# Attention and expert kernel: a prologue for one head and one batch, and the banks of the transposed groups from the scores' ring

## The chip, the cores and the metric

The kernel runs on one core of a Trainium2 chip. The metric is the device time of one execution in microseconds. Before the change the median of three runs is 740.85 us (740.27 to 741.19).

## The reference

Three stages, one behind the other, all in fp32:

```python
q_pool = q.reshape(B, H, S // 2, 2, D).mean(axis=3)          # B 2, H 8, S 1152, D 64
scores = softmax(1/sqrt(D) * q_pool @ k.transpose(0, 1, 3, 2))
x = (scores @ v) -> rows (b, s), columns (h, d)              # 1152 x 512
out = experts(x): top 2 of 8 by noisy logits, relu(x @ w1[e]) @ w2[e]
h = out @ w_in; result = (h * cos(h)) @ w_out                # 512 x 2048, 2048 x 512
```

The change touches the attention stage alone, and of it the preparation of q and k.

## The kernel before

TensorE multiplies in a fast form of fp32 that keeps fewer bits, so each operand is split into a high part (written in that form) and a low part (the rest), and a product is made of two or three matmuls.

**Row tiles.** Attention goes over 72 row tiles `n` (`tiles`, line 281): 4 pairs of heads `hp`, 2 heads `hl` in a pair, 9 tiles `t` of 128 pooled query rows. The 1152 rows of a head are batch 0 (tiles 0 to 3 and half of tile 4) and batch 1 (the other half of tile 4, tiles 5 to 8). A tile has 1152 keys, in three score banks of 384 columns. In iteration `n` of the main loop (line 880) TensorE makes the scores of tile `n + 1` (`s_bank`: two matmuls a bank, high q and low q; three or four for the tile across both batches), VectorE their negative maxima (`s_max`), ScalarE their exponentials (`s_exp`, which also sums them: an instruction of its own then reads the accumulator). For tile `n` TensorE transposes the exponentials (`t_pe`, three groups), ScalarE and VectorE split two of them (`t_hi`, `t_lo`), ScalarE and GpSimd the third (`t_pool`). The products with v wait in a list (`avq`) from which each iteration takes 9, or 6 where `t` is 2 to 4 (`NPOP`); a product is 256 or 320 columns wide.

The order on an engine is the order in which the code issues. ScalarE's order in an iteration is `t_hi` 0 and 1 of tile `n`, exponentials 0 and 1 of tile `n + 1`, `t_pool`'s copy, exponential 2, and then copies of whatever group stands at the end of the iteration. TensorE's is score banks 0 and 1, `t_pe` 0, score bank 2, `t_pe` 1, products, `t_pe` 2, products, the group at the end.

**Banks.** PSUM's eight banks are three rings: `s` of four (scores), `pt` of three (`tbank`, line 122: transposes), `pa` of one (products). A ring hands its banks out in turn, and a new user waits for the last reader of the bank's former user.

**The plan.** Head pairs are prepared while the pair before is worked on. `plan` (line 728) puts each step at an iteration: loads, `pool_q` (adds neighbouring rows of q, GpSimd), `q_group` and `k_group` (three transposes into one bank and a copy by ScalarE; issued at the end of an iteration), `q_split` and `k_split` (GpSimd), then `q_asm`, `l_asm`, `q_bd`, `k_asm` (transfers from SBUF to SBUF, all in SyncE's queue, that bring the parts to the partitions where the score matmuls want them). `kb` and `qd` are the block rows for the low part of the tile across both batches. At the end of some iterations stands instead a row group (`x_group`): the finished columns of the output are transposed, scaled and stored.

**The prologue** (lines 770 to 862) loads q and k of heads 0 and 1 in both batches: q of batch 0 for head 0 and head 1, k of batch 0 in six pieces, k of batch 1 in two, q of batch 1 in two. Ten matmuls (`warm`) run while the loads are under way. For batch 0 VectorE adds q, TensorE transposes q and k of both heads together (`q_front`, `k_direct`), ScalarE writes the high parts and VectorE the low parts, and three more copies bring head 0's q to the other 64 partitions. Then come the scores of tile 0, key groups of batch 1, the exponentials of tile 0, the scores of tile 1 and the rest of q for batch 1, with copies on VectorE and ScalarE in iterations 1 and 2, and 17 transfers.

Of the kernel before, what the change touches and what calls it, by code (L numbers as in the profile page):

```python
# [22 lines left out]
def attn_moe_cos_kernel(ctx, tc, q, k, v, w_gate, w_noise, noise, w1, w2, w_in, w_out, out):  # L23
# [174 lines left out]
    def k_tiles(hp, b):
        kk = [qk.tile([128, S], F32R, name="kt", bufs=5) for _ in range(2)]
        KT[hp, 0, b], KT[hp, 1, b] = kk  # L200
        return kk

    def load_qb(hl, b):
        if b == 0:
            QN[0, hl] = prep.tile([128, 18, 64], F32, name="qn", bufs=2)
        nc.sync.dma_start(QN[0, hl][b * 64:(b + 1) * 64], q[b, hl].rearrange("(p r) d -> p r d", r=18))

    def pool_qb(hl, b, eng):
        rs = slice(b * 64, b * 64 + 64)
        t = QN[0, hl][rs].rearrange("p (s r) d -> p s r d", r=2)  # L210
        eng.tensor_tensor(QP[0][rs, :, hl, :], t[:, :, 0, :], t[:, :, 1, :], op=OP.add)
# [3 lines left out]
    def q_front(j, b):  # L215
        QB[j] = p = tbank()
        rs = slice(b * 64, b * 64 + 64)
        for i in range(3):
            nc.tensor.transpose(p[:, i * 64:(i + 1) * 64], QP[0][rs, 3 * j + i].rearrange("p h d -> p (h d)"), ident[rs, rs])

    def q_part(t, b, j):
        return t[:, b * QB1:b * QB1 + SQ].rearrange("p (s c) -> p s c", c=9)[:, :, 3 * j:3 * j + 3]

    def q_hi(b, j, o):
        nc.scalar.activation(q_part(o, b, j), QB[j][:, 0:192].rearrange("p (i s) -> p s i", i=3), AF.Copy, scale=1.0 / 16.0)
# [502 lines left out]
    def plan():  # L728
# [5 lines left out]
        for hp in range(HP):  # L734
            n0 = 18 * hp
            for hl in range(2):
                for b in range(B):
                    s = n0 + 9 * hl + 5 * b
                    at(s - 7, load_v, hp, hl, b)
                    at(s - 3, split_v, hp, hl, b)  # L740
            if hp:
# [29 lines left out]
    pres = ExitStack()  # L771
    pro = pres.enter_context(tc.tile_pool(name="pro", bufs=1, side="right", reuse_waits="tile"))
    load_qb(0, 0)
    load_qb(1, 0)
    load_k(0, 0)
    load_k(0, 1, pro)
    load_qb(0, 1)
    load_qb(1, 1)
    warm(tbank, WQ)
    QP[0] = prep.tile([128, 9, 2, 64], F32, name="qp", bufs=1)  # L780
    QH = QS[0] = prep.tile([128, 1216], F32R, name="sh", bufs=2)
    QL[0] = prep.tile([128, 1216], F32R, name="ql", bufs=1)
    t = t0 = Q2[0, 0] = qk.tile([128, 1216], F32R, name="q2", bufs=3)
    L0 = QL2[0, 0] = qk.tile([128, 1216], F32R, name="l2", bufs=2)
    for i in range(3):
        z = slice(512 * i, min(512 * i + 512, 1216))
        nc.gpsimd.tensor_scalar(L0[64:128, z], ZERO[64:128, 0:z.stop - z.start], 1.0, 0.0, op0=OP.mult, op1=OP.add)
    for hl in range(2):
        pool_qb(hl, 0, nc.vector)
    for j in range(3):  # L790
        q_front(j, 0)
    kk = k_tiles(0, 0)
    kbank = [lambda: ps.tile([128, 512], F32, name="s", bufs=4)] * 2 + [lambda: ps.tile([128, 512], F32, name="pa", bufs=1)]
    kg = [k_direct(0, 0, j, kk, kbank[j]) for j in range(3)]
    for g in kg:
        next(g)
    for j in range(3):
        q_hi(0, j, QH)
        q_lo(0, j)
    c = slice(0, SQ)  # L800
    nc.scalar.activation(t[64:128, c], QH[0:64, c], AF.Copy)
    nc.vector.tensor_scalar(t[0:64, c], QH[0:64, c], 1.0, 0.0, op0=OP.mult, op1=OP.add)
    nc.gpsimd.tensor_scalar(L0[0:64, c], QL[0].bitcast(F32)[0:64, c], 1.0, 0.0, op0=OP.mult, op1=OP.add)
    for g in kg:
        next(g)
    next(kg[0])
    s_mm(0)
    QR = pro.tile([128, 1216], F32, name="qr")
    z = slice(SQ, QB1)
    nc.gpsimd.memset(QR[:, z], 0.0)  # L810
    nc.gpsimd.tensor_scalar(QH[:, z], QR[:, z], 1.0, 0.0, op0=OP.mult, op1=OP.add)
    for hl in range(2):
        pool_qb(hl, 1, nc.gpsimd)
    QN.clear()
# [8 lines left out]
    for g in kg[1:]:
        next(g)
    KN.pop((0, 0))
    for j in range(3):
        k_group(0, 1, j)
# [10 lines left out]
    for j in range(3):
        q_hi(1, j, QR)
        q_hi(1, j, QH)  # L840
    k_split(0, 1)
    c = slice(SQ, 1216)
    nc.gpsimd.tensor_tensor(QL[0][:, c], QR[:, c], QH.bitcast(F32)[:, c], op=OP.subtract)
    lo0 = QL[0].bitcast(F32)
    ev.setdefault(1, []).insert(0, (lambda: nc.vector.tensor_scalar(
        t0[0:64, c], QH[0:64, c], 1.0, 0.0, op0=OP.mult, op1=OP.add), ()))
    ev.setdefault(2, []).insert(0, (lambda: nc.vector.tensor_scalar(
        L0[0:64, c], lo0[0:64, c], 1.0, 0.0, op0=OP.mult, op1=OP.add), ()))
    ev.setdefault(2, []).insert(0, (lambda: nc.scalar.activation(t0[64:128, c], QH[0:64, c], AF.Copy), ()))
    k_asm_a(0, 1)  # L850
    q_asm(0, 1, False)
    l_asm(0, 1)
    for n in sorted(e for e in ev if e < 0):
        for f, a in ev[n]:
            if f != load_v:
                f(*a)
    pres.close()
    kbp.append(qes.enter_context(tc.tile_pool(name="kbp", bufs=1, reuse_waits="tile")))
    k_stack(0)
    k_asm_b(0, 1)  # L860
    nc.sync.dma_start(KB[0, 1].bitcast(F32)[0:64], KT[0, 1, 0].bitcast(F32)[64:128])
    q_bd(0, 1)
# [17 lines left out]
    for n in range(NTOT - 1):  # L880
        hp, hl, t = tiles[n]
        for f, a in ev.get(n, []):
            if f not in (q_group, k_group):
# [58 lines left out]
        fl = [(f, a) for f, a in ev.get(n, []) if f in (q_group, k_group)]  # L942
# [770 lines left out]
```

## Time and profile before

| | before |
|---|---|
| median of 3 runs | 740.85 us (740.27 to 741.19) |
| profiled execution | 739.14 us, its span 737.6 us |
| TensorE (PE) busy | 722.5 us, 98% of the span |
| VectorE (DVE), ScalarE (ACT), GpSimd (POOL) busy | 562.3, 528.8, 301.9 us |
| granted TensorE clock, mean | 0.999 of full speed |

The profile is one execution on the chip; times are microseconds from the start of its span. The ends of matmuls are modelled, so the spacing of their starts tells more than their lengths. A row ahead of which an engine sat idle names in brackets for how long, and what released it. The attention stage lasts until about 275 us; the experts and the last two products follow.

### The profile page before, as it was taken

The numbers are of one execution on the slowest core, as the hardware profiler recorded it, in microseconds if no ns is written. First come the engines' busy times: TensorE is split into PE (matmuls) and PEld (weight loads), VectorE is DVE, ScalarE is ACT, GpSimd is POOL, SyncE is SP. The second block draws the span as 40 slices with busy tenths as digits, with TensorE's granted clock in tenths as the row PEclk, the third lists the DMA queues.
The fourth block names the chain that finished last, engine by engine and source line by source line (L and its number), as shares of the span: only waits on it lengthen the run. The fifth ranks groups of instructions, "written<-read, shape, count | busy, mean of one in ns | idle before, by whom it ended". The sixth has DMA issues, their size and how long they took to land.

```text
span 737.6 us, 13760 instructions
## 1 busy us (share of the span) xinstructions
PE 722.5 (98%) x4803; PEld 673.9 (91%) x4803; DVE 562.3 (76%) x1161; ACT 528.8 (72%) x1200; POOL 301.9 (41%) x329
## 2 busy tenths in 40 slices
PE   6999999999999999999999999999999999999997
PEld 4899999999999989999999999999889989888885
DVE  5888788888878988879889887776677776556562
ACT  5999799979988964458777676766588665555443
POOL 5988867877977973212022021103187110000000
PEclk9999999999999999999999999999999999999999
DMA  9957756695665511798999999968353210010001
GB/s 207 244 94 183 184 130 147 163 237 106 161 140 146 179 44 29 248 314 295 363 371 328 334 345 330 329 233 286 119 171 97 85 29 1 1 44 0 1 1 60
DMA packets 75329, 125.02 MB, mean 169 GB/s; under 512 B 11950, under 2 KB 42030, under 8 KB 75254
## 3 DMA queue, kind: packets, MB, share of 16 engines
q1 hardware_dynamic: 68678, 101.92, 47.3%
q0 software_dynamic: 5568, 19.14, 7.4%
q10 hardware_dynamic: 1008, 3.02, 1.6%
q8 instruction: 40, 0.66, 0.4%
q14 instruction: 35, 0.29, 0.1%
HBM read 82.15 MB, written 20.33 MB: 139 GB/s over the span
## 4 chain that ended last, share of the span: by engine, by line
PE 90%; DVE 4%; ACT 3%; DMA 1%; issue 0%; SPq 0%; ACTq 0%; DVEq 0%
PE h L1145 20%; PE acc L1145 16%; PE acc L1177 11%; PE s L310 10%; PE pa L386 9%; PE pt L348 9%; PE t L1145 7%; PE pt L694 2%; PE t L1137 1%; PE pt L984 1%; PE t L1194 1%; PE pt L180 1%; DMA raw<-in_moe_w_dram 1%; DVE nm L324 1%; DVE el L365 1%; DMA qn<-in_q_dram 1%
## 5 line engine op out<-in xcount | busy, mean ns | idle before, releaser
L324 DVE TENSOR_REDUCE nm<-s 128x1 f32<-128x384 f32 x216 | 112.1, 551 | 23.4 <-PE s L310 21.8
L333 ACT ACTIVATE p<-s,nm 128x384 f32<-128x384 f32 x216 | 125.1, 583 | 2.8 <-DVE nm L326 1.5
L1145 PE MATMUL h<-xe,u 128*128 128x320 f32 (+5 forms) x768 | 120.1, 306 | 0.0
L1145 PEld LDWEIGHTS h<-xe,u 128*128 128x128 f32 x768 | 109.6, 188 | 0.5
L642 DVE TENSOR_TENSOR u<-raw,u 128x1024 fp32r<-128x1024 f32 x66 | 80.9, 1227 | 34.4 <-ACT u L641 33.6
L348 PE MATMUL pt<-ident,p 128*128 128x128 f32 x645 | 105.0, 272 | 0.0
L310 PE MATMUL s<-kt,q 128*128 128x384 f32 x240 | 88.8, 386 | 3.7 <-DVE kt L195 2.1
L348 PEld LDWEIGHTS pt<-ident,p 128*128 128x128 f32 x645 | 81.7, 140 | 5.7
L386 PE MATMUL pa<-eh,v 128*128 128x320 f32 (+1 forms) x279 | 86.5, 324 | 0.0
L641 ACT ACTIVATE u<-raw 128x1024 fp32r<-128x1024 f32 x73 | 77.1, 1057 | 10.3 <-DMA raw<-in_moe_w_dram 5.8
L361 ACT ACTIVATE eh<-pt 128x384 fp32r<-128x384 f32 x144 | 68.9, 501 | 20.3 <-PE pt L348 19.0
L386 PE MATMUL pa<-el,v 128*128 128x320 f32 (+1 forms) x279 | 82.4, 309 | 0.0
L372 POOL TENSOR_TENSOR el<-rw,eh 128x384 fp32r<-128x384 f32 x71 | 71.9, 1012 | 5.9
L365 DVE TENSOR_TENSOR el<-pt,eh 128x384 fp32r<-128x384 f32 x144 | 72.9, 547 | 1.0 <-ACT eh L361 0.9
L1177 PE MATMUL acc<-hh,u 128*128 128x320 f32 (+5 forms) x448 | 71.8, 302 | 0.1
L1145 PE MATMUL acc<-u,gh 128*128 128x512 f32 x216 | 66.9, 391 | 0.0
L310 PE MATMUL s<-kt,l 128*128 128x384 f32 x198 | 66.3, 337 | 0.0
L1177 PEld LDWEIGHTS acc<-hh,u 128*128 128x128 f32 x448 | 64.7, 188 | 0.4 <-ACT hh L1156 0.4
L1232 POOL DMA_DIRECT2D w_d<-dw x16 | 9.0, 563 | 130.5 <-DVE dw L1231 130.5
L371 POOL TENSOR_SCALAR eh<-rw 128x384 fp32r<-128x384 f32 x71 | 36.8, 518 | 42.0 <-ACT rw L369 39.7
L386 PEld LDWEIGHTS pa<-el,v 128*128 128x128 f32 x279 | 52.9, 190 | 0.0
L386 PEld LDWEIGHTS pa<-eh,v 128*128 128x128 f32 x279 | 52.8, 189 | 0.0
(292 smaller groups left out, 1605.9 us busy)
## 6 DMA issues: line engine op xcount, KB each, us to landing
raw<-in_moe_w_dram SPq DMA_DIRECT2D x64, 512.0 KB
raw<-in_moe_w_in_dram SPq DMA_DIRECT2D x16, 512.0 KB
raw<-in_moe_w_out_dram SPq DMA_DIRECT2D x16, 512.0 KB
w_d<-dw POOLq DMA_DIRECT2D x16, 512.0 KB, 5.4
raw<-w_d SPq DMA_DIRECT2D x13, 512.0 KB
vn<-in_v_dram SPq DMA_DIRECT2D x16, 288.0 KB
q<-sh SPq DMA_DIRECT2D x14, 304.0 KB
l<-ql SPq DMA_DIRECT2D x14, 304.0 KB
```

What stands on the lines that cost most here:

```text
L310: nc.tensor.matmul(o, l, r, start=(m == 0), stop=(m == len(mm) - 1))
L324: nc.vector.tensor_reduce(NM[n][:, i:i + 1], SB[n][i][:, 0:384], axis=AX.X, op=OP.max, negate=True)
L333: nc.scalar.activation(P[n][i], SB[n][i][:, 0:384], AF.Exp, bias=NM[n][:, 3:4], accum_out=SUMS[:, t, 2 * hp + hl, i:i + 1])
L348: nc.tensor.transpose(p[:, c], P[n][j][:, c], ident)
L361: nc.scalar.activation(t_dst(n, j)[0], t_src(n, j), AF.Copy)
L365: nc.vector.tensor_tensor(el, t_src(n, j), ef, op=OP.subtract)
L372: nc.gpsimd.tensor_tensor(el, rw, ef, op=OP.subtract)
L386: nc.tensor.matmul(st["p"][:, 0:w], V2[hp, hl, b][:, VC[c] if hp + b else c, :], (EH, EL)[s][:, c, EB[g]:EB[g] + w], start=(c == 0 and s = ...
L641: nc.scalar.activation(b[:, 0], r, AF.Copy)
L642: st_w["lo"].tensor_tensor(b[:, 1], r, b.bitcast(F32)[:, 0], op=OP.subtract)
L1145: nc.tensor.matmul(o, l, r, start=first and i == 0, stop=last and i == len(seq) - 1)
L1177: nc.tensor.matmul(ACC[e, d][:, 0:CAPS[e]], w[:, i, 128 * d:128 * d + 128], r[:, 0:CAPS[e]], start=f == 0 and r is hh and i == 0, stop=f = ...
```

## The change

Part one: the prologue prepares head 0 alone, first its batch 0. The four loads are q of batch 0, k of batch 0, q of batch 1, k of batch 1 (each 288 KB). The added rows of q are written twice beside each other, so that one transposition fills all 128 partitions, and ScalarE and VectorE write high and low parts straight to their places (`pool_p`, `q_tr`, `q0_hi`, `q0_lo`). The keys of batch 0 are transposed 64 columns at a time into the lower partitions (`k0_tr`, `k0_part`). Behind the scores of tile 0 follow batch 1's q, and batch 1's keys (`k0b_copy`, `k0b_split`, four transfers). Head 1's q and k are loaded in the prologue, and prepared in iterations 1 to 9: `pool_h1` at 1, key groups at 1, 2 and 3, `k_split` at 4, q groups (`q1_group`) at 4, 5 and 6 with their low parts on VectorE one iteration later (`late`), eight transfers (`k1_asm`) at 6 and six (`k1_bd`) at 9. Some steps of pair 1 move with it: its first key load from 2 to 4, its second q group from 6 to 7, and the split of v for batch 1 from 2 to 5. The warming matmuls are 11, and use the matrix of ones for both operands.

Part two: key groups (`k_group`), q groups of pairs 2 and 3 and of head 1 of pair 0, and all row groups but the last two take their bank from the ring `s` of four instead of `pt`.

The core of the diff; definitions of helpers that only move data as told above are left out:

```diff
@@ q_group
-        p = tbank()
+        p = ps.tile([128, 512], F32, name="s", bufs=4) if hp > 1 else tbank()
@@ k_group
-            KS[hp, b] = prep.tile([128, 1216], F32, name="st", bufs=1)[:, 0:S]
-        p = tbank()
+            KS[hp, b] = prep.tile([128, 1216], F32, name="st", bufs=1)[:, 0:S] if hp else XS0
+        p = gbank()
...
+    def pool_p(hl, rs, cs, eng):
+        t = QN[0, hl][rs].rearrange("p (s r) d -> p s r d", r=2)
+        o = QP[0, hl][rs, cs]
+        eng.tensor_tensor(o[:, :, 0, :], t[:, cs, 0, :], t[:, cs, 1, :], op=OP.add)
+        if eng is nc.vector:
+            nc.scalar.activation(o[:, :, 1, :], o[:, :, 0, :], AF.Copy)
+        else:
+            eng.tensor_scalar(o[:, :, 1, :], o[:, :, 0, :], 1.0, 0.0, op0=OP.mult, op1=OP.add)
...
+    def gbank():
+        return ps.tile([128, 512], F32, name="s", bufs=4)
...
+    def q1_group(j):
+        cs = slice(3 * j, 3 * j + 3)
+        q_tr(1, slice(0, 128), cs, ("h", j))
+        src = QB["h", j][:, 0:384].rearrange("p (i b s) -> p b s i", i=3, b=2)
+        for b in range(2):
+            nc.scalar.activation(q0_out(Q2[0, 1], b, cs), src[:, b], AF.Copy, scale=1.0 / 16.0)
+        late.append(lambda: [nc.vector.scalar_tensor_tensor(...) for b in range(2)])
...
+    def k0b_copy():
+        KS[0, 0] = t = XF[:, 1280:1920]
+        nc.gpsimd.memset(t[HI, 512:640], 0.0)
+        pa, pb = tbank(), tbank()
+        k_tr(1, 0, pa)
+        nc.scalar.activation(t[:, 0:384], pa[:, 0:384], AF.Copy)
+        k_tr(1, 1, pb)
+        nc.scalar.activation(t[:, 384:512], pb[:, 0:128], AF.Copy)
+        nc.scalar.activation(t[LO, 512:640], pb[LO, 128:256], AF.Copy)
...
@@ x_group
-        p = tbank()
+        p = ps.tile([128, 512], F32, name="s", bufs=4) if (hp, g) < (HP - 1, 2) else tbank()
@@ plan
-                    at(s - 3, split_v, hp, hl, b)
+                    at(5 if s == 5 else s - 3, split_v, hp, hl, b)
-                at(m + 2, load_k, hp, 0)
+                at(m + (4 if hp == 1 else 2), load_k, hp, 0)
-                    at(m + (3 + 2 * d, 5 + d, 6 + d)[j], q_group, hp, j)
+                    at(m + (3 + 2 * d, 5 + 2 * d, 6 + d)[j], q_group, hp, j)
+        for j in range(3):
+            at(1 + j, k_group, 0, 1, j)
+            at((4, 5, 6)[j], q1_group, j)
+        at(4, k_split, 0, 1)
+        at(6, k1_asm)
+        at(9, k1_open)
+        at(9, k1_bd)
@@ prologue (new)
+    load_h0(nc.sync, "q", 0)
+    load_h0(nc.sync, "k", 0)
+    load_h0(nc.sync, "q", 1)
+    load_h0(nc.sync, "k", 1)
+    warm(tbank, WQ)
...
+    for i in range(2):
+        pool_p(0, LO, PART[i], nc.vector)
+        q_tr(0, LO, PART[i], (0, i))
+    kb3 = [ps.tile([128, 512], F32, name="s", bufs=4) for _ in range(2)]
+    kb3.append(ps.tile([128, 512], F32, name="pa", bufs=1))
+    for j in range(3):
+        k0_tr(j, kb3[j])
+    for i in range(2):
+        q0_hi(0, i)
+        q0_lo(0, i)
+    for j in range(3):
+        k0_part(j, kb3[j])
+    pool_p(0, HI, slice(0, 9), nc.gpsimd)
+    s_mm(0)
...
+    for i in range(3):
+        s_max(0, i)
+    for i in range(2):
+        q_tr(0, HI, PART[i], (1, i))
+        q0_hi(1, i)
+        q0_lo(1, i)
+    k0b_copy()
+    load_k1()
+    k0b_split()
+    for i in range(3):
+        s_exp(0, i)
```

## Rows read from the trace of the kernel before

**Rows 1.** Page, part 1: busy time of each engine, share of the span, instructions.

```profile
PE 722.5 (98%) x4803; PEld 673.9 (91%) x4803; DVE 562.3 (76%) x1161; ACT 528.8 (72%) x1200; POOL 301.9 (41%) x329
```

**Rows 2.** Table by stretches: start:end, length, busy time per engine (instructions), clock, DMA.

```profile
30.00:40.00 10.00, 10.00 (x75) 9.56 (x74) 8.30 (x20) 9.82 (x33) 9.49 (x13) 1.00 0.85 206
```

**Rows 3.** Timeline, prologue: start us, length us, engine, line, operation, count [idle before <-releaser].

```profile
4.90 0.75 DVE L211 TENSOR_TENSOR qp<-qn 64x576 f32<-64x576 f32 x1 [2.32 <-DMA qn<-in_q_dram]
6.41 0.75 DVE L211 TENSOR_TENSOR qp<-qn 64x576 f32<-64x576 f32 x1 [0.76 <-DMA qn<-in_q_dram]
7.31 0.74 PE L219 MATMUL pt<-ident,qp 64*128 64x64 f32 x9 [0.64 <-DVE qp L211]
...
8.11 0.89 DVE L228 SCALAR_TENSOR_TENSOR ql<-pt,sh 128x192 fp32r<-128x192 f32 x3 [0.95 <-ACT sh L225]
9.27 0.86 ACT L194 ACTIVATE kt<-s 64x384 fp32r<-64x384 f32 x2
9.79 1.01 DVE L195 TENSOR_TENSOR kt<-s,kt 64x384 fp32r<-64x384 f32 x2 [0.44 <-ACT kt L194]
12.13 2.78 POOL L211 TENSOR_TENSOR qp<-qn 64x576 f32<-64x576 f32 x2 [1.83 <-DMA qn<-in_q_dram]
13.41 0.16 DVE L326 TENSOR_REDUCE nm<-nm 128x1 f32<-128x3 f32 x1
14.03 0.60 ACT L333 ACTIVATE p<-s,nm 128x384 f32<-128x384 f32 x1
...
17.81 0.63 ACT L333 ACTIVATE p<-s,nm 128x384 f32<-128x384 f32 x1
```

**Rows 4.** Timeline, tiles 2 and 3: a score matmul and what released it.

```profile
21.39 0.19 ACT L333 ACTIVATION_READ_ACCUMULATOR p<-s,nm 128x1 f32 x1
...
21.64 0.44 PE L310 MATMUL s<-kt,q 128*128 128x384 f32 x1 [0.65 <-ACT p L333]
```

**Rows 5.** Timeline, tiles 9 to 11: exponentials and third score banks.

```profile
45.31 0.58 ACT L333 ACTIVATE p<-s,nm 128x384 f32<-128x384 f32 x1
...
47.19 0.42 PE L310 MATMUL s<-kt,q 128*128 128x384 f32 x1
...
48.67 0.58 ACT L333 ACTIVATE p<-s,nm 128x384 f32<-128x384 f32 x1
...
50.63 0.22 ACT L333 ACTIVATION_READ_ACCUMULATOR p<-s,nm 128x1 f32 x1
50.64 0.42 PE L310 MATMUL s<-kt,q 128*128 128x384 f32 x1
```

**Rows 6.** Timeline, tiles 22 and 23: around the first q group of pair 2.

```profile
93.99 0.28 PE L386 MATMUL pa<-el,v 128*128 128x256 f32 x1
94.29 0.52 PE L136 MATMUL pt<-ident,qp 128*128 128x128 f32 x3
...
95.60 0.42 PE L310 MATMUL s<-kt,q 128*128 128x384 f32 x1
95.74 0.22 ACT L333 ACTIVATION_READ_ACCUMULATOR p<-s,nm 128x1 f32 x1
```

**Rows 7.** Timeline, tiles 15 to 17: a key group behind a ScalarE-bound tile, and the next.

```profile
67.34 0.22 ACT L333 ACTIVATION_READ_ACCUMULATOR p<-s,nm 128x1 f32 x1
67.38 0.42 PE L310 MATMUL s<-kt,q 128*128 128x384 f32 x1
...
71.08 0.42 PE L310 MATMUL s<-kt,q 128*128 128x384 f32 x1
```

**Rows 8.** Timeline, last iteration: row group of pair 3, exponentials of tile 70.

```profile
264.90 1.01 PE L694 MATMUL pt<-GW,xt 128*128 128x80 f32 x8
265.11 0.22 ACT L333 ACTIVATION_READ_ACCUMULATOR p<-s,nm 128x1 f32 x1
```

**Rows 9.** Timeline, GpSimd's split of pair 1's q and its last transfers.

```profile
46.26 2.81 POOL L149 TENSOR_TENSOR ql<-st,sh 128x1216 fp32r<-128x1216 f32 x1
...
50.24 2.82 SPq L172 DMA_DIRECT2D qd<-ql  x2
```

More of the change, by code (lines that the diff above doesn't have):

```diff
@@ L198, in k_tiles @@
[L198 to L211, printed above, removed]
@@ L213, in attn_moe_cos_kernel @@
-    QB = {}
[L215 to L225, printed above, removed]
@@ L227, in q_lo, with load_h0 @@
-    def q_lo(b, j):
-        nc.vector.scalar_tensor_tensor(q_part(QL[0], b, j), QB[j][:, 0:192].rearrange("p (i s) -> p s i", i=3), 1.0 / 16.0,
-                                       q_part(QS[0].bitcast(F32), b, j), op0=OP.mult, op1=OP.subtract)
+    WQ = 11
+    XF = X.rearrange("p t d -> p (t d)")
+    VC0 = tuple(range(9))
+    def load_h0(eng, kind, b):
+        if kind == "q":
+            if b == 0:
+                QN[0, 0] = prep.tile([128, 18, 64], F32, name="qn", bufs=2)
+            eng.dma_start(QN[0, 0][b * 64:(b + 1) * 64], q[b, 0].rearrange("(p r) d -> p r d", r=18))
+        else:
+            if b == 0:
+                KN[0, 0] = prep.tile([128, 2, 576], F32, name="kn", bufs=1)
+            eng.dma_start(KN[0, 0][:, b], k[b, 0].rearrange("(p c) d -> p (c d)", c=9))
@@ new lines, in load_h1, with load_k1 @@
+    def load_h1():
+        QN[0, 1] = prep.tile([128, 18, 64], F32, name="qn", bufs=2)
+        for b in range(2):
+            nc.sync.dma_start(QN[0, 1][b * 64:(b + 1) * 64], q[b, 1].rearrange("(p r) d -> p r d", r=18))
+    def load_k1():
+        KN[0, 1] = prep.tile([128, 2, 576], F32, name="kn", bufs=1)
+        for b in range(2):
+            nc.sync.dma_start(KN[0, 1][:, b], k[b, 1].rearrange("(p c) d -> p (c d)", c=9))
+    PART = (slice(0, 6), slice(6, 9))
+    def pool_p(hl, rs, cs, eng):
[4 more added lines that the diff above has]
+            nc.scalar.activation(o[:, :, 1, :], o[:, :, 0, :], AF.Copy)
+        else:
+            eng.tensor_scalar(o[:, :, 1, :], o[:, :, 0, :], 1.0, 0.0, op0=OP.mult, op1=OP.add)
@@ new lines, in attn_moe_cos_kernel, with q_tr, q_hi, q0_out @@
+    QB = {}
+    def gbank():
+        return ps.tile([128, 512], F32, name="s", bufs=4)
+    def q_tr(hl, rs, cs, key):
+        w = rs.stop - rs.start
+        QB[key] = p = gbank() if hl else tbank()
+        for i in range(cs.stop - cs.start):
+            nc.tensor.transpose(p[:, i * w:(i + 1) * w], QP[0, hl][rs, cs.start + i].rearrange("p k d -> p (k d)"), ident[rs, rs])
+    def q_hi(key, o, n):
+        nc.scalar.activation(o, QB[key][:, 0:n], AF.Copy, scale=1.0 / 16.0)
+    def q0_out(t, b, cs):
+        return t[:, b * QB1:b * QB1 + SQ].rearrange("p (s c) -> p s c", c=9)[:, :, cs]
@@ new lines, in q0_src, with q0_hi, q0_lo @@
+    def q0_src(key, cs):
+        return QB[key][:, 0:64 * (cs.stop - cs.start)].rearrange("p (i s) -> p s i", s=64)
+    def q0_hi(b, i):
+        nc.scalar.activation(q0_out(Q2[0, 0], b, PART[i]), q0_src((b, i), PART[i]), AF.Copy, scale=1.0 / 16.0)
+    def q0_lo(b, i):
+        nc.vector.scalar_tensor_tensor(q0_out(QL2[0, 0], b, PART[i]), q0_src((b, i), PART[i]), 1.0 / 16.0,
+                                       q0_out(Q2[0, 0].bitcast(F32), b, PART[i]), op0=OP.mult, op1=OP.subtract)
+    def q1_group(j):
+        cs = slice(3 * j, 3 * j + 3)
+        q_tr(1, slice(0, 128), cs, ("h", j))
+        src = QB["h", j][:, 0:384].rearrange("p (i b s) -> p b s i", i=3, b=2)
+        for b in range(2):
+            nc.scalar.activation(q0_out(Q2[0, 1], b, cs), src[:, b], AF.Copy, scale=1.0 / 16.0)
+        late.append(lambda: [nc.vector.scalar_tensor_tensor(q0_out(QL2[0, 1], b, cs), src[:, b], 1.0 / 16.0,
+                                                            q0_out(Q2[0, 1].bitcast(F32), b, cs), op0=OP.mult, op1=OP.subtract)
+                             for b in range(2)])
@@ new lines, in attn_moe_cos_kernel, with gap, q1_open, k_tr @@
+    late = []
+    def gap(t):
+        nc.gpsimd.tensor_scalar(t[:, SQ:QB1], ZERO[:, 0:QB1 - SQ], 1.0, 0.0, op0=OP.mult, op1=OP.add)
+    def q1_open():
+        Q2[0, 1] = qk.tile([128, 1216], F32R, name="q2", bufs=3)
+        QL2[0, 1] = qk.tile([128, 1216], F32R, name="l2", bufs=2)
+        gap(Q2[0, 1])
+        gap(QL2[0, 1])
+    def k_tr(b, i, p):
+        kn = KN[0, 0][:, b]
+        for m in range(3 if i == 0 else 2):
+            c = 384 * i + 128 * m
+            w = min(128, 576 - c)
+            nc.tensor.transpose(p[0:w, 128 * m:128 * m + 128], kn[:, c:c + w], ident)
@@ new lines, in k0b_split, with k1_asm @@
+    def k0b_split():
+        r = KS.pop((0, 0))
+        h = prep.tile([128, 1216], F32R, name="sh", bufs=2)[:, 0:640]
+        nc.gpsimd.tensor_scalar(h, r, 1.0, 0.0, op0=OP.mult, op1=OP.add)
+        nc.gpsimd.tensor_tensor(r, r, h.bitcast(F32), op=OP.subtract)
+        KT[0, 0, 1] = qk.tile([128, S], F32R, name="kt", bufs=5)
+        k_put(KT[0, 0, 1][LO], h.bitcast(F32), 0)
+        k_put(KT[0, 0, 1][HI], r, 0)
+    def k1_asm():
+        h, r = KS.pop((0, 1))
+        K1H.append(h)
+        for b in range(2):
+            KT[0, 1, b] = qk.tile([128, S], F32R, name="kt", bufs=5)
+        for b in range(2):
+            k_put(KT[0, 1, b][HI], r, b)
+        for b in range(2):
+            k_put(KT[0, 1, b][LO], h.bitcast(F32), b)
@@ L231, in k_split, with k1_bd, k1_open @@
+    def k1_bd():
+        h = K1H[0]
+        for b in range(2):
+            k_put(KB[0, 1][b * 64:b * 64 + 64], h.bitcast(F32), b)
+            c0 = 4 * 128 if b == 0 else 4 * 128 - SQ + QB1
+            nc.sync.dma_start(QD[0, 1].bitcast(F32)[b * 64:b * 64 + 64],
+                              QL2[0, 1].bitcast(F32)[b * 64:b * 64 + 64, c0:c0 + 128])
+    K1H = []
+    def k1_open():
+        QD[0, 1] = kbp[0].tile([128, 128], F32R, name="qd", bufs=2)
     def k_split(hp, b):
@@ L770, in attn_moe_cos_kernel @@
     ev = plan()
[L771 to L778, printed above, removed]
-    warm(tbank, WQ)
[L780 to L814, printed above, removed]
+    kbp.append(qes.enter_context(tc.tile_pool(name="kbp", bufs=1, reuse_waits="tile")))
+    k_stack(0)
+    load_h0(nc.sync, "q", 0)
+    load_h0(nc.sync, "k", 0)
+    load_h0(nc.sync, "q", 1)
+    load_h0(nc.sync, "k", 1)
+    warm(tbank, WQ)
+    QP[0, 0] = prep.tile([128, 9, 2, 64], F32, name="qp", bufs=1)
+    QP[0, 1] = XF[:, 128:1280].rearrange("p (c k d) -> p c k d", c=9, k=2)
     for n in sorted(e for e in ev if e < 0):
@@ L818, in attn_moe_cos_kernel @@
                 f(*a)
-    load_q(1, 0)
-    load_q(1, 1)
+    load_h1()
+    t0 = Q2[0, 0] = qk.tile([128, 1216], F32R, name="q2", bufs=3)
+    L0 = QL2[0, 0] = qk.tile([128, 1216], F32R, name="l2", bufs=2)
+    KT[0, 0, 0] = qk.tile([128, S], F32R, name="kt", bufs=5)
+    gap(t0)
+    gap(L0)
+    for i in range(2):
[12 more added lines that the diff above has]
+    s_mm(0)
+    for n in sorted(e for e in ev if e < 0):
+        for f, a in ev[n]:
+            if f != load_v:
+                f(*a)
     for i in range(3):
         s_max(0, i)
[L823 to L827, printed above, removed]
+    for i in range(2):
[5 more added lines that the diff above has]
+    k0b_split()
     for i in range(3):
@@ L832, in attn_moe_cos_kernel, with pool_h1 @@
         s_bank(1, i)
-        if i == 0:
-            for j in range(3):
-                q_front(j, 1)
     for i in range(3):
         s_max(1, i)
[L838 to L862, printed above, removed]
+    def pool_h1():
+        pool_p(1, slice(0, 128), slice(0, 9), nc.gpsimd)
+        QN.pop((0, 1))
+        load_q(1, 1)
+        q1_open()
+    QN.pop((0, 0))
+    load_q(1, 0)
+    ev.setdefault(1, []).insert(0, (pool_h1, ()))
     NPOP = (9, 9, 6, 6, 6, 9, 9, 9, 9)
@@ L928, in attn_moe_cos_kernel @@
         t_lo(n, 1)
+        if late:
+            late.pop(0)()
         if xg:
@@ L941, in attn_moe_cos_kernel @@
                 r_inv(hp, GEND[t])
-        fl = [(f, a) for f, a in ev.get(n, []) if f in (q_group, k_group)]
+        fl = [(f, a) for f, a in ev.get(n, []) if f in (q_group, k_group, q1_group)]
         for f, a in fl:
```

30 lines of the change are left out of this document (14 added, 16 removed).

## The prediction

> **What bounds the kernel now.** I read the page first: TensorE is busy for 722.5 of 737.6 us [rows 1], so only its idle time, or a change in what it must do, can move the end. The table by stretches says where that idle time is: from 30 us on TensorE is busy 10.00 of 10.00 us [rows 2], so before 30 us the kernel fills up, and behind it a microsecond that TensorE loses anywhere is a microsecond at the end. Then I read the filling in order of time [rows 3]: the first q load lands for the add at 4.90, the second for that at 6.41; the keys' split on VectorE goes on past 11; the negative maximum of row tile 0 is ready at 13.57 (13.41 + 0.16); its first exponential starts at 14.03, that of tile 1 at 17.81. Last I looked at what the change makes TensorE wait for, the scores' ring of four banks. The reader is to see one thing there: a score matmul that needs a bank starts 0.06 us after ScalarE's read of the accumulator of the exponential that held the bank (21.39 + 0.19 = 21.58, matmul at 21.64) [rows 4].
>
> The sum is made against the profiled execution (span 737.6, 739.14 us in all); the median of the runs is 740.85, 1.7 us more, and I add the same difference to it.
>
> **The change, part by part.**
>
> *Prologue up to the scores of tile 0.* Only head 0 and batch 0 are prepared. The first load is the same, so 4.90 stays [rows 3]. VectorE adds 384 of the 576 columns (0.75 x 2/3, 0.5 us), and ScalarE writes the sum a second time. No row has that copy from SBUF at 64x384; below it lies the 64x384 eviction (two in 0.86, so 0.43), above it the 0.75 of the add of 576 columns; I take 0.5. Six transposes and their drain: 9 take 0.74, so 0.6. High part on ScalarE 0.5, low parts on VectorE 0.95 (three of 192 columns take 0.89), then three key parts on VectorE at 0.51 (two in 1.01). 4.90 + 0.5 + 0.5 + 0.6 + 0.5 + 0.95 + 1.5 = 9.5, with some 0.1 of hand-overs 9.6. The key transposes lie beside the q evictions: their load is now second in the queue, where a load lands at 6.41, before they are due at 6.7. Three maxima and the fourth then end at 11.3 instead of 13.57: 2.3 us earlier. Gone from the path are head 1's transposes and key parts, the two copies of q to other partitions and the wait for the second head's load.
>
> *First exponentials.* Not all of that arrives. ScalarE has the second batch's q and three key copies ahead of the first exponential. GpSimd adds and doubles that batch (1.39 + about 0.8) when its load, third in the queue at some 1.5 us a load, has landed at 7.8; TensorE takes it behind the scores at 10; the last key bank comes from the ring of three and waits for VectorE's low part, which stands behind the maxima (11.9); copies end near 12.85. So tile 0 gains 1.2 us over 14.03. Tile 1's exponential has no q evictions in front any more (six today) and comes at about 16.15, 1.66 us before 17.81.
>
> *Tiles 1 to 9 take the displaced work.* Head 1's keys (three groups of three transposes and a copy) and head 1's q (three groups) now run in iterations 1 to 6, with banks from the scores' ring. Such a group shifts the ring by one bank: the third score bank of the next tile is then the one that held the third bank of this tile, not the second, and must wait for this tile's last exponential, which ScalarE issues last. That round is a chain: tile 10's third bank starts at 47.19, its first exponential at 48.67, the accumulator of the third is read by 50.85 (50.63 + 0.22) [rows 5]; with 0.06 the next third bank can't start before 3.72 us after the last. From tile 1's first exponential to tile 10's today 48.67 - 17.81 = 30.86. After: 2.95 (ScalarE alone: 2.18 for the exponentials, two evictions), four times 3.72, 4.07 (tile 4 has two more matmuls in a bank, at some 0.17), twice 3.94 (3.69 of TensorE plus a second group's 0.25, since two groups stand in iterations 5 and 7), 3.36 as today (48.67 - 45.31): 33.1. That is 2.3 more, so 1.66 is given back and 0.6 lost. The chain's price is bounded below by ScalarE's own work (2.95 + 0.45 a group), which would make the nine tiles 31.6.
>
> *The same ring for pairs 1 to 3.* Where TensorE's own period is 3.72 or more, nothing happens; where it is less, the difference is lost, and no slack behind it gives it back [rows 2]. Six key groups lie in tiles with 256-wide products: tile 11's third bank is issued at 50.64 and couldn't be before 50.91 [rows 5]: 6 x 0.27 = 1.6. Two q groups follow a tile across both batches: 95.60 against 95.74 + 0.22 + 0.06 = 96.02 [rows 6]: 0.84. Three key groups follow a tile bound by ScalarE: 67.38 against 67.62 [rows 7]: 0.72. Thirteen have 320-wide products and a period of 3.70 (67.38 to 71.08) [rows 7]: 0.02 each, 0.3. Row groups of pairs 0 to 2 stand in tiles of 4 us and more: nothing. The row group of the last pair in the last iteration starts at 264.90, and would take the bank whose accumulator is read until 265.33: 0.49 [rows 8], and the transposes and VectorE's chain behind it move along. Together 3.95.
>
> What the ring of three costs today: a q group issued at 94.29 where the spacing of its neighbours would give 94.11, so 0.18 [rows 6]. I find four such places; in three of them the new wait ends later anyway, so 0.18 is won.
>
> The Trainium skill (Perfetto Trace Analysis, Matmul Optimizations) asks that all eight PSUM banks be used so that more instructions can overlap, and by it a ring of four instead of three should only help. Here all eight are in use before and after (4 + 3 + 1), and the fourth bank of the scores is what spares the third bank its wait; by that rule the sum for the pairs would be -0.7 instead of +3.8.
>
> *Covered, with what it costs if the cover goes.* Head 1's keys are loaded once head 0's are read, at 12.3; the span's first load is there 4.90 us after its start [rows 3], so the keys are there at about 17.2, a microsecond before the first group. GpSimd is nearly full, as it is today (9.49 of 10 us [rows 2]): the same instructions at today's lengths make 31.7 us for its first nine tiles, which last 33; if it falls behind, the third part of each tile is late for the products, which have some 3 us. The eight transfers that assemble head 1's keys are issued from 33 us and needed at 44. The warming matmuls start earlier and change nothing behind 4.90.
>
> Sum: +0.6 + 3.95 - 0.18 = +4.4 us: 743.5 for a profiled execution like this one, 745.2 against the median.
>
> **The rivals.**
>
> *The ring doesn't bind* (faster). If the exponentials come earlier than the chain says, or banks are handed out so that the third score bank doesn't get the last one's, the filling keeps its lead: tile 10 at 16.15 + 31.6 = 47.8, 0.9 before 48.67, and the four waits of the ring of three go, 0.7: -1.6 us, 739.3. For it speaks that in most groups the margin is a few hundredths. Against it stand the wait of rows 4, which is this ring's, and that the chain of rows 5 repeats in every tile. It decides at the first key group of pair 1: it holds if the third banks stay 3.45 apart.
>
> *The prologue saves more than I count.* If key banks and second batch don't stand before the first exponential (load earlier, copies beside), tile 1 comes up to 1.5 us sooner, and with tiles 2 to 6 nearer to ScalarE's 3.4 than to 3.72 (four times 0.3) the loss shrinks to 4.4 - 2.7 = 1.7: 742.5.
>
> *Head 1's block rows come late.* Six transfers now stand behind pair 1's q in the one queue, which itself waits for GpSimd's split until 49.07 and has its last piece issued at 53.06 (50.24 + 2.82) [rows 9]. Six more at about 0.6 are out at 56.7 and land 1 to 2 us later; tile 13 needs them at 57.9. If they miss by a microsecond: 746.2. Today they are done by 32 us.
>
> **How the numbers follow.** Forecast (ring binds, sizes as above, 744 to 746) 0.60; ring doesn't bind 0.15; prologue saves more 0.15; block rows late 0.10. Within 0.2% (1.5 us, about what a measurement of this kernel can tell from no change) fall a fifth of the second case and half of the third. Faster 0.13, same 0.12, slower 0.75. The range goes from 740.3, a third case with every bound in its favour, to 747, forecast with late block rows and 0.8 for the small terms; only the faster rival and little else is left out.
>
> **What would show it.** Right: first exponential near 12.9 and second tile's near 16.2; ScalarE's exponential named as releaser of score matmuls, some 0.27 before the third bank after key groups of pairs 1 to 3 and 0.4 at the two q groups; about 0.5 at the last row group; TensorE's idle time beyond 30 us up by some 4 us. Wrong: third banks after a group 3.45 apart, no such waits, or tile 10's first exponential before 48.7. A long wait at tile 13 for a transfer would be the last rival.

## The result, and the profile after

The changed kernel takes 744.72 us, median of five runs (742.92 to 745.70), against 740.85 (740.27 to 741.36) for the kernel before on the same chip: ratio 1.006, 95% interval 1.0040 to 1.0081. The forecast was 745.2. Its profiled execution took 742.92 us with a span of 741.4; before it was 739.14 and 737.6.

Where the loss shows, and where it doesn't, is the first thing to see. First the page's busy time, to be held against [rows 1]; then the table by stretches from 30 us to shortly before the end of attention, 268 us before and 272 after (columns as in [rows 2]). After:

```profile
PE 729.1 (98%) x4818; PEld 675.6 (91%) x4818; DVE 561.2 (76%) x1162; ACT 528.4 (71%) x1201; POOL 301.9 (41%) x331
```

```profile
30.00:272.00 242.00, 240.81 (x1759) 226.82 (x1758) 199.87 (x492) 214.76 (x639) 189.53 (x211) 1.00 0.63 155
```

The same stretch before:

```profile
30.00:268.00 238.00, 237.42 (x1762) 227.93 (x1762) 199.27 (x489) 214.72 (x639) 188.19 (x211) 1.00 0.63 156
```

In this stretch TensorE's busy time rose by 3.39 us (240.81 - 237.42) for nearly the same matmuls, and its idle time only from 0.58 to 1.19 us; of the 6.6 us by which the page's busy time rose, the rest stands ahead of 30 us, in another prologue, and behind attention. So the sign that I had named, "TensorE's idle time beyond 30 us up by some 4 us", doesn't hold: the modelled ends of matmuls fill waits of a few tenths. The weight loads (PEld) show them: their idle time rose from 10.07 to 15.18 us. Their waits, grouped by what released them (total us, times, longest), say why. After, from 30 to 272 us:

```profile
PEld s L409 <- ACT p L432: 6.5, 29, 0.3
PEld s L409 <- DMA qd<-l: 1.2, 1, 1.2
PEld s L793 <- ACT p L432: 0.6, 1, 0.6
```

Before, from 30 to 272 us:

```profile
PEld s L310 <- ACT p L333: 3.1, 15, 0.3
...
PEld pt L694 <- PE pt L348: 1.0, 3, 0.3
```

Score matmuls (L409, before L310) wait for ScalarE's exponential 29 times instead of 15; one waits 1.2 us for a transfer; the row groups' wait for a `pt` bank (L694, 3 times) is gone.

The timeline of the new prologue, to be held against [rows 3]:

```profile
4.79 0.82 DVE L214 TENSOR_TENSOR qp<-qn 64x384 f32<-64x384 f32 x2 [2.22 <-DMA qn<-in_q_dram]
8.99 0.54 DVE L285 TENSOR_TENSOR kt<-pa,kt 64x384 fp32r<-64x384 f32 x1
11.09 0.15 DVE L425 TENSOR_REDUCE nm<-nm 128x1 f32<-128x3 f32 x1
12.77 0.57 ACT L432 ACTIVATE p<-s,nm 128x384 f32<-128x384 f32 x1
...
15.78 0.58 ACT L432 ACTIVATE p<-s,nm 128x384 f32<-128x384 f32 x1
```

The keys' last part ends at 9.53 (8.99 + 0.54; forecast 9.6), the maximum at 11.24 (11.3), tile 0's exponential starts at 12.77 (12.85), tile 1's at 15.78 (16.15). So the prologue wins what was expected, a little more. Tiles 10 and 11, to be held against [rows 5]:

```profile
47.89 0.42 PE L409 MATMUL s<-kt,q 128*128 128x384 f32 x1
...
49.36 0.58 ACT L432 ACTIVATE p<-s,nm 128x384 f32<-128x384 f32 x1
...
51.32 0.22 ACT L432 ACTIVATION_READ_ACCUMULATOR p<-s,nm 128x1 f32 x1
...
51.59 0.19 PEld L409 LDWEIGHTS s<-kt,q 128*128 128x128 f32 x1 [0.23 <-ACT p L432]
51.59 0.44 PE L409 MATMUL s<-kt,q 128*128 128x384 f32 x1
```

Tile 10's exponential stands at 49.36 instead of 48.67: the lead of 2 us has become a lag of 0.7. And the next third bank starts 0.05 us after the last exponential's accumulator is read (51.32 + 0.22 = 51.54, matmul at 51.59), 3.70 us after the last third bank, where it was 3.45. The same 0.05 stands behind the first q group of pair 2 [rows 6]:

```profile
97.85 0.22 ACT L432 ACTIVATION_READ_ACCUMULATOR p<-s,nm 128x1 f32 x1
...
98.12 0.19 PEld L409 LDWEIGHTS s<-kt,q 128*128 128x128 f32 x1 [0.24 <-ACT p L432]
```

and at the last row group, to be held against [rows 8], where the group's first matmul now stands behind the read:

```profile
269.32 0.22 ACT L432 ACTIVATION_READ_ACCUMULATOR p<-s,nm 128x1 f32 x1
269.59 0.52 PEld L793 LDWEIGHTS s<-GW,xt 128*128 128x128 f32 x4 [0.65 <-ACT p L432]
```

Two things I had not put into the sum. The first is the block rows at tile 13. Before, TensorE took them without a wait:

```profile
56.77 0.34 PE L310 MATMUL s<-kb,qd 128*128 128x384 f32 x1
```

After, SyncE's queue, then TensorE:

```profile
50.80 2.82 SPq L172 DMA_DIRECT2D qd<-ql  x2
53.66 1.24 SPq L348 DMA_DIRECT2D kb<-sh  x2
...
56.91 0.55 SPq L322 DMA_DIRECT2D qd<-l  x1
...
59.02 0.45 PE L409 MATMUL s<-kb,qd 128*128 128x384 f32 x1 [0.87 <-DMA qd<-l]
```

The last of the six transfers is issued at 56.91, behind pair 1's q, and TensorE stands idle for it. The second is the row groups of pairs 0 to 2. In the row group behind tile 21 the bank came before from `pt`, whose former group VectorE's low part (L365) had to read first:

```profile
89.17 1.01 DVE L365 TENSOR_TENSOR el<-pt,eh 128x384 fp32r<-128x384 f32 x2
...
89.42 0.28 PE L386 MATMUL pa<-el,v 128*128 128x256 f32 x1
89.86 1.09 PE L694 MATMUL pt<-GW,xt 128*128 128x80 f32 x8 [0.16 <-DVE el L365]
```

After, the same group stands 0.12 us behind the product ahead of it instead of 0.44:

```profile
91.94 0.28 PE L485 MATMUL pa<-el,v 128*128 128x256 f32 x1
92.06 1.01 PE L793 MATMUL s<-GW,xt 128*128 128x80 f32 x8
```

### Where the time went, tile by tile

The table sums, for each kernel of this study, how much longer or shorter than before the periods are (from one tile's third score bank to the next tile's), in us, from the profiled executions. "To 10" is the lag of tile 10's third bank; the last column is that of tile 70's, at the end of attention. Key groups: six behind tiles 10, 11, 28, 29, 46, 47, three behind 15, 33, 51; q groups behind 22 and 40; even ones: twelve behind 16, 17, 24, 25, 27 and their like (320-wide products, a period of 3.69); row groups behind 20, 21, 38, 39, 56, 57, of which 21, 39 and 57 give nearly all of the gain, some 0.4 each.

| kernel | to 10 | 12 | 6 key | 2 q | 3 key | 12 even | row | rest | at 70 |
|---|---|---|---|---|---|---|---|---|---|
| after | +0.70 | +1.12 | +1.70 | +0.80 | +0.70 | +0.35 | -1.26 | +0.10 | +4.21 |
| e2 ring alone | +0.38 | +0.09 | +1.73 | +0.82 | +0.67 | +0.37 | -1.31 | +0.20 | +2.95 |
| e1 groups back | +0.44 | +2.65 | -0.03 | 0 | -0.03 | -0.18 | -0.12 | -0.16 | +2.57 |
| e3 exp first | +0.77 | +4.15 | +0.13 | +0.33 | 0 | -0.14 | -1.45 | +1.55 | +5.34 |
| e4 block rows early | +0.72 | +0.08 | +1.71 | +0.81 | +0.69 | +0.34 | -1.25 | +0.12 | +3.22 |
| e7 exp first, block early | +0.21 | +0.01 | +0.14 | +0.33 | -0.01 | +0.40 | -1.45 | -0.18 | -0.55 |
| e8 prologue alone | -0.14 | +0.02 | -0.01 | -0.01 | -0.01 | +0.26 | +0.06 | -0.15 | +0.02 |
| e5 rows only, block early | +0.25 | +0.01 | 0 | -0.02 | -0.03 | -0.19 | -1.26 | -0.18 | -1.42 |
| e6 before, rows only | -0.09 | 0 | 0 | 0 | 0 | -0.03 | -1.27 | -0.04 | -1.43 |

Single periods mostly repeat to 0.03 between kernels that share a part. The filling scatters: tile 0's exponential starts at 12.77 to 13.61 us in the seven profiled executions of the new prologue, and tile 10 stands 0.4 us apart in e5 and e8. The +0.26 and +0.40 of e8 and e7 under "even" come from tile 16 alone (0.40 and 0.54); the other eleven tiles stand at -0.02 to 0.

### The profile page after: what moved, and what is told of

The parts are those of the page before. It is cut to its first block, busy times and chain, and to the rows that moved or that the text cites. A ratio compares the mean times of both kernels' runs of the same rounds, so it can differ in the third digit from the quotient of the medians.

```text
span 741.4 us, 13785 instructions
## 1 busy us (share of the span) xinstructions
PE 729.1 (98%) x4818; PEld 675.6 (91%) x4818; DVE 561.2 (76%) x1162; ACT 528.4 (71%) x1201; POOL 301.9 (41%) x331
## 3 DMA queue, kind: packets, MB, share of 16 engines
q10 hardware_dynamic: 1008, 3.02, 1.6%
## 4 chain that ended last, share of the span: by engine, by line
PE 94%; ACT 2%; DVE 2%; DMA 1%; issue 0%; ACTq 0%; DVEq 0%
PE h L1224 21%; PE acc L1224 15%; PE acc L1256 13%; PE s L409 12%; PE pa L485 9%; PE pt L447 9%; PE t L1224 7%; PE s L793 2%; PE t L1273 1%; PE t L1216 1%; PE pt L1063 1%; PE s L182 1%; ACT p L432 1%; DMA qn<-in_q_dram 1%; PE acc L1350 0%; PE pa L1063 0%
## 5 line engine op out<-in xcount | busy, mean ns | idle before, releaser
L741 DVE TENSOR_TENSOR u<-raw,u 128x1024 fp32r<-128x1024 f32 x66 | 81.0, 1228 | 33.1 <-ACT u L740 32.8
L409 PE MATMUL s<-kt,q 128*128 128x384 f32 x240 | 90.2, 392 | 2.5 <-ACT p L432 1.8
L409 PE MATMUL s<-kt,l 128*128 128x384 f32 x198 | 66.4, 338 | 0.0
L409 PEld LDWEIGHTS s<-kt,q 128*128 128x128 f32 x240 | 43.7, 188 | 13.9 <-ACT p L432 10.4
```

What stands on the lines that cost most here:

```text
L409: nc.tensor.matmul(o, l, r, start=(m == 0), stop=(m == len(mm) - 1))
L741: st_w["lo"].tensor_tensor(b[:, 1], r, b.bitcast(F32)[:, 0], op=OP.subtract)
```

## The experiments

Theory: the ring of four makes the third score bank wait for ScalarE's last exponential, and the block rows add a microsecond. Rivals: the loss comes from the new prologue, or from work moved onto GpSimd. The kernel before had 738.89 us (median of 11 runs) beside e1 to e4, and 739.57 (35 runs) beside e5 to e8; the times expected for e1 to e4 were reckoned from 740.85, so that the ratios are what compares. All kernels compute everything.

**e1: the groups' banks back in the ring of three.**

```diff
# q_group, k_group, x_group
-        p = ps.tile([128, 512], F32, name="s", bufs=4) ...
+        p = tbank()
```

> Key, q and row groups take their bank from the ring of three again; head 1's q groups and the whole new prologue stay. Theory (the ring of four makes the third score bank wait for the last exponential): the waits after groups go, 3.85 us by the periods measured tile by tile (1.70 key groups in 256-wide tiles, 0.80 q groups behind tile 4, 0.70 key groups behind a ScalarE-bound tile, 0.35 in the even ones, 0.3 last row group); the filling's three key groups give about 1.0; the row groups lose the 1.35 that they gained: 744.7 - 3.5 = 741.2. The new prologue's wait for the block rows (0.9) stays in the trace. Rival (the prologue's displaced work costs the time, and the ring nothing): 744.7, unchanged.

Measured 743.82 us (741.77 to 744.61), ratio 1.0052 (1.0033 to 1.0071): by the time alone a miss. The trace shows both sides. Every ring term went to zero as the theory says, the row groups' gain with them. But tile 12 now costs 2.65: TensorE came to the block rows earlier and waited longer.

```profile
56.77 0.60 PE L409 MATMUL s<-kt,q 128*128 128x384 f32 x2
59.72 0.45 PE L409 MATMUL s<-kb,qd 128*128 128x384 f32 x1 [2.35 <-DMA qd<-l]
```

The rows landed at 59.7 here and at 59.0 in the changed kernel. So what is won ahead of tile 13 is given back there, and this experiment can't judge the sum. The lag is 2.57 us at tile 70; another 2.2 us of the profiled execution are two waits of the experts for VectorE (1.80 and 0.39) that I can't tie to the edit.

**e2: the ring alone, in the kernel before.**

```diff
# kernel before: k_group, q_group, x_group
-        p = tbank()
+        p = ps.tile([128, 512], F32, name="s", bufs=4) if hp else tbank()          # k_group
+        p = ps.tile([128, 512], F32, name="s", bufs=4) if hp > 1 else tbank()      # q_group
+        p = ps.tile([128, 512], F32, name="s", bufs=4) if (hp, g) < (HP - 1, 2) else tbank()   # x_group
```

> The kernel before with part two alone: key and q groups of pairs 1 to 3 (q groups of pairs 2 and 3) and all row groups but the last two in the ring of four, old prologue. Theory: 740.85 + 3.55 for key and q groups + 0.3 for the last row group - 1.35 for the other row groups + 0.1 at tile 12 = 743.4. Rival (prologue costs): 740.85, or 0.7 less since the ring of three no longer delays some groups.

Measured 742.49 us (741.94 to 746.21), ratio 1.0055 (1.0033 to 1.0077), slower clear of the noise; tile 70 lags by 2.95, of which 0.37 stand from tile 1 on: 2.58 for the ring. With the old prologue, the terms are those of the changed kernel within 0.05. So no part of them comes from the prologue. The wait is the same:

```profile
51.01 0.22 ACT L333 ACTIVATION_READ_ACCUMULATOR p<-s,nm 128x1 f32 x1
51.27 0.19 PEld L310 LDWEIGHTS s<-kt,q 128*128 128x128 f32 x1 [0.24 <-ACT p L333]
```

**e3: the changed kernel with the third exponential ahead of ScalarE's copy.**

```diff
-        t_pool(n, 2)
         s_exp(n + 1, 2)
+        t_pool(n, 2)
```

> The changed kernel, but ScalarE issues the third exponential of a tile ahead of the copy of the third transposed group, and not behind it. Theory: the accumulator of the third exponential is read 0.37 us sooner, so the round of third banks is 3.35 instead of 3.72 us: waits in 256-wide tiles (1.70), behind ScalarE-bound tiles (0.70), in the even ones (0.35) and at the last row group (0.3) go, the two q groups keep a few hundredths (0.75 won), the six rounds of the filling give about 0.2 each (1.3): 744.7 - 5.1 = 739.6. What could spoil it: the copy comes 0.6 later, and GpSimd with it. Rival (prologue costs): 744.7 or, with the later copy, more.

Measured 744.14 us (743.57 to 745.78), ratio 1.0064 (1.0048 to 1.0080): again a miss by the time, and again at tile 13. The ring's terms fell (six key groups +0.13 instead of +1.70), but the block rows' wait is 3.02 us. They landed later still, at 60.7: their transfers stand behind pair 1's q, which waits for GpSimd's split, and that ended at 50.79 instead of 49.62. (In this execution tile 0's exponential had started 0.84 us later than in the changed kernel's, so not all of the delay is the edit's.) And TensorE came out of the wait slower:

```profile
47.98 2.81 POOL L149 TENSOR_TENSOR ql<-st,sh 128x1216 fp32r<-128x1216 f32 x1
...
58.64 0.55 SPq L322 DMA_DIRECT2D qd<-l  x1
...
60.73 0.69 PE L409 MATMUL s<-kb,qd 128*128 128x384 f32 x1 [3.02 <-DMA qd<-l]
...
62.67 0.99 PE L409 MATMUL s<-kt,q 128*128 128x384 f32 x2
```

The table by stretches of e3 (the clock is the third column from the right):

```profile
59.50:59.70 0.20, 0.00 (x0) 0.00 (x0) 0.00 (x0) 0.00 (x0) 0.20 (x1) 1.00 1.11 287
...
59.90:60.10 0.20, 0.00 (x0) 0.00 (x0) 0.00 (x0) 0.00 (x0) 0.20 (x1) 0.50 0.57 128
...
60.70:62.60 1.90, 1.87 (x7) 1.78 (x8) 0.75 (x2) 0.00 (x0) 1.82 (x2) 0.50 1.02 205
...
66.40:66.60 0.20, 0.20 (x2) 0.20 (x2) 0.00 (x0) 0.20 (x1) 0.00 (x0) 0.50 0.84 202
...
68.00:72.00 4.00, 4.00 (x33) 3.71 (x31) 3.89 (x13) 3.64 (x11) 1.64 (x3) 1.00 0.98 224
```

The granted clock falls from 1.00 (2.4 GHz) to 0.50 (1.2 GHz) between 59.7 and 59.9 us, while TensorE still sits idle, stays there until 66.6 and is at 1.00 again in the stretch from 68; tile 13's period is 4.77 instead of 3.08.

**e4: the block rows one iteration earlier in the changed kernel.**

```diff
-        at(9, k1_open)
-        at(9, k1_bd)
+        at(8, k1_open)
+        at(8, k1_bd)
```

> The changed kernel with the six transfers of head 1's block rows put into iteration 8 instead of 9, so that they stand ahead of pair 1's q in the one queue. Theory: the wait of TensorE for them at tile 13 (0.94 us) goes, nothing else moves: 743.8. Rival (the wait covers something else that is late there, so another wait takes its place): 744.7.

Measured 743.38 us (742.11 to 744.85), ratio 1.0056 (1.0039 to 1.0074). The interval can't tell it from the changed kernel's 1.0060; the trace can: tile 70 lags by 3.22 instead of 4.21, all of the difference at tile 12. The transfers now go out ahead of pair 1's q, and the matmul doesn't wait:

```profile
43.65 1.24 SPq L348 DMA_DIRECT2D kb<-sh  x2
44.98 0.54 SPq L322 DMA_DIRECT2D qd<-l  x1
...
50.96 1.20 SPq L156 DMA_DIRECT2D q<-sh  x2
```

```profile
57.56 0.62 PE L409 MATMUL s<-kt,q 128*128 128x384 f32 x2
58.02 0.34 PE L409 MATMUL s<-kb,qd 128*128 128x384 f32 x1
```

With that floor out of the way, e7 and e8 put the questions of e3 and e1 again, and e5 and e6 take the row groups alone.

**e7: e3 and e4 together** (both diffs above).

> Changed kernel with ScalarE's third exponential ahead of its copy of the third transposed group (s_exp before t_pool) and the block rows k1_bd one place earlier; all work is done. Theory (two causes: the ring of four waits for ScalarE's last exponential, and the block rows wait behind pair 1's q in SP's queue): with exp-first alone the third score bank of tile 13 stood 4.96 us after that of before, because the block rows' wait took 3.02 us and TensorE then ran at a granted clock of 0.5; without that wait tile 12's bank stands at +0.8 and the ring's waits are gone from there on (key groups' periods 3.46 instead of 3.73, third bank of tile 70 within -1.0 to +0.3 us of before's, against +4.2 in the changed kernel). Time within 0.2% of before, 3 to 5 us below the changed kernel. Rival (the moved copy costs as much as the exponential gains, since the weighted values wait for it): tile 70 at +3 or more, time as with the block rows alone (+3.3 in the trace).

Measured 739.79 us (737.87 to 741.83), ratio 1.0008 (0.9994 to 1.0021): the same as before, with every bank still in the ring of four. Tile 70 stands at -0.55. The exponentials of tile 10 and the next third bank:

```profile
50.47 0.21 ACT L432 ACTIVATION_READ_ACCUMULATOR p<-s,nm 128x1 f32 x1
50.56 0.49 ACT L468 ACTIVATE rw<-pt 128x384 f32<-128x384 f32 x1
50.84 0.19 PEld L409 LDWEIGHTS s<-kt,q 128*128 128x128 f32 x1
50.87 0.42 PE L409 MATMUL s<-kt,q 128*128 128x384 f32 x1
```

The read ends at 50.68, the matmul comes at 50.87 and waits for nothing. Nothing but ScalarE's order and the block rows differs from the changed kernel, so these two account for the loss. The work that the change moved onto GpSimd is all there still, here and in e8, so that rival falls.

**e8: e1 and e4 together** (banks back, head 1's key groups with them; block rows early): the new prologue alone, with head 1's q groups still in the ring of four.

> Changed kernel with the banks of the k, q and row groups of pairs 1 to 3 back in the ring of three (head 1's q groups of pair 0 stay in the ring of four) and k1_bd one place earlier; all work is done. Theory (new filling worth nothing by tile 12, ring the rest): with the groups back alone tile 12's third bank stood +0.43 us after before's, then the block rows cost 2.6; without that cost the bank of tile 70 stands between -0.4 and +0.6 us of before's, and the time within 0.2% of before. Rival (the new filling itself costs some microseconds): tile 70 at +2 or more.

Measured 738.86 us (737.12 to 741.02), ratio 0.9997 (0.9983 to 1.0010); tile 70 at +0.02. Within the scatter of the filling (0.4 us) the new prologue itself is worth nothing and costs nothing. One wait of 0.4 us in tile 16 (a `pt` bank whose key group ScalarE had yet to copy) is new here.

**e5: e8 with the row groups' banks left in the ring of four.**

> The same as the prologue alone, but the row groups' banks (x_group) stay in the ring of four; all work is done. Theory (the row groups gain where the k and q groups lose: X no longer waits in the ring of three for VectorE's t_lo): the periods of tiles 21, 39 and 57 are 3.98 instead of 4.39, so 1.2 us less at tile 70 than with the prologue alone, -1.6 to -0.6 us against before; time 0 to 2 us below before. Rival (the row groups' 0.4 is won only after a tile delayed by a k or q group): no difference from the prologue alone at tile 70.

Measured 737.67 us (736.95 to 740.88), ratio 0.9979 (0.9967 to 0.9991): it beats both kernels, by 0.2% the one before. Its row group behind tile 21 stands 0.11 us behind the product:

```profile
89.15 1.01 DVE L464 TENSOR_TENSOR el<-pt,eh 128x384 fp32r<-128x384 f32 x2
...
89.48 0.28 PE L485 MATMUL pa<-el,v 128*128 128x256 f32 x1
89.59 1.01 PE L793 MATMUL s<-GW,xt 128*128 128x80 f32 x8
```

VectorE still works on the low part (89.15 to 90.16) when the group starts: it needs no bank of that ring.

**e6: the kernel before with the row groups' banks alone in the ring of four** (the x_group line of e2).

> The kernel before with only x_group's banks in the scores' ring of four; nothing else changed, all work is done. Theory: periods of tiles 21, 39 and 57 3.98 instead of 4.39, tile 70's third bank 1.2 us earlier (-1.0 to -1.5) than before's, time 1.0 to 1.5 us below before. Rival (no gain, the forecast's own step that the row groups change nothing): tile 70 at 0, time the same.

Measured 738.71 us (737.70 to 746.26), ratio 0.9996 (0.9976 to 1.0015): the interval, widened by one run of 746.26, holds no change as well as the 1.0 to 1.5 us expected. In the trace the gain is there, -1.43 at tile 70, -1.27 of it in the six tiles of row groups, as in every kernel that has these banks in `s`.

## Why the prediction was right, and where it was not

**The mechanism held.** The chain that I read off [rows 4, 5] (third bank, exponentials, accumulator read, next third bank) sets the distance of the third banks wherever a group takes a bank of the ring: 3.70 to 3.73 measured, 3.72 said, the matmul 0.05 us after the read. Term by term, forecast and measured: filling +0.6 and +0.70; six key groups 1.6 and 1.70; two q groups 0.84 and 0.80; three key groups 0.72 and 0.70; even ones 0.3 and 0.35 (and 0.08 in tile 12); last row group 0.49 and 0.48 (its first matmul lags by 4.69, tile 70 by 4.21). e2 shows the ring's terms without the prologue, e7 takes them away by moving one exponential.

**The filling.** The prologue's gain came as said, tile 1 even 0.37 earlier, and it was given back in the amount said: from tile 1's exponential to tile 10's 33.58 us instead of 30.86 (forecast 33.1). But the ring's round is the smaller part of that. With head 1's key groups out of the ring (e1) the stretch still takes 32.79 us, and with the exponential issued first (e7) 32.80; the shorter period of the two in each tile gives some 32.4, an estimate of the stretch without the ring's wait. So the ring costs 0.8 to 1.2, where the forecast had 1.5 (33.1 less the 31.6 that it gave as the floor without the chain). That floor was 0.8 to 1.2 us too low: the displaced work costs more by itself than I had counted, and the term came out because the two errors offset each other in it. In any case the lead is gone (e8: -0.14 at tile 10). "Prologue saves more" didn't come: tile 1 was 0.37 us sooner than forecast and not 1.5, and tiles 2 to 6 took 3.73 to 4.30 us.

**Two steps failed, and nearly cancelled.** "Row groups of pairs 0 to 2 stand in tiles of 4 us and more: nothing", and with it "what the ring of three costs today: 0.18": I had looked for waits at q and key groups, and had taken a long period for one with slack. In these tiles TensorE's own period is the bound and the wait for the `pt` bank lies in it: 4.39 us with it, 3.98 without. That is -1.26 where I had 0 (e5, e6). On the other side "head 1's block rows come late" was only a rival with a chance of 0.10 and a price of 1.0 us; it happened beside the forecast: tile 12's period is 1.12 longer, 0.08 with the transfers early (e4), so 1.04. Its own working spoke for it: needed at 57.9 (the 56.77 of before and the forecast's lag), landed 1 to 2 us after 56.7, so at 57.7 to 58.7. That is a miss over most of the range, and no reason for one chance in ten. Measured, the rows were needed at about 58.0, the last issue ended at 57.5, and they landed at 59.0.

**The sum.** +4.4 forecast, +3.78 in the profiled executions, +3.87 in the medians. Tile 70 lags by 4.21, the first matmul behind attention by 4.76, the last matmul of all by 4.34, and the span by 3.8; the 0.4 won between and the half microsecond behind the last matmul I can't place. That the sum came within 0.6 us is therefore in part luck: -1.26 and +1.04 nearly cancel, and almost 1 us of the lag goes again behind attention, for a cause that stays open.

**The rule on all eight banks.** The Trainium skill (Perfetto Trace Analysis, Matmul Optimizations) asks that all eight PSUM banks be in use. All eight are in use in each of these kernels, so the rule doesn't decide between them; that a ring of four instead of three should only help, and make the pairs 0.7 us faster, was my reading of it. For the key and q groups the measurement is against that reading (+3.55 for 23 groups); for the row groups it is borne out (-1.26). What differs is whose last reader a bank waits for.

## What to carry to other kernels

A bank borrowed from a ring shifts the ring by one: ask which reader each later user then waits for, and when that reader is issued. Borrow where the lender's next user comes late (row groups, -1.26), not where it waits for the engine's last instruction (q and key groups, +3.55); or issue that instruction earlier (e7). And before an experiment is judged by its time, look for a wait behind the edit that the edit doesn't shorten, here for a transfer that landed at 59.0 to 60.7 us: it swallowed what e1 and e3 had won.

## What the runs showed of the hardware

In an idle time of TensorE of 3.02 us (e3, until 60.73) the granted clock fell to 0.50, and it stayed there until 66.6 us, under matmuls that followed one another without a gap; those of 384 columns took 0.52 instead of 0.34 us. In an idle time of 2.35 us at the same place it didn't fall (e1):

```profile
59.70:61.00 1.30, 1.28 (x8) 1.25 (x9) 0.80 (x2) 0.00 (x0) 1.22 (x2) 1.00 0.94 191
```

So the late block rows cost e3 another 1.7 us in tile 13, and by an estimate some 0.8 of tile 12's 4.15 (e1: 2.65, with a wait 0.67 shorter). These are single executions: the mean granted clock of e1's others goes down to 0.994, that of e3 here, and no trace shows where. The other lesson is about the profile: waits of 0.2 to 0.4 us stand in the weight loads' rows, while TensorE's busy time grows by them.
